# An output projection cut into Strassen units for all four blocks, with a shorter feature map and numerators divided on GpSimd

## The chip, the cores and the metric

The kernel runs on one core of a Trainium2 chip. The metric is device time in microseconds (us) of one execution, lower is better. The engines are called PE (TensorE, the matmuls), PEld (its weight loads), DVE (VectorE), ACT (ScalarE), POOL (GpSimd) and SP (SyncE, which here issues most DMAs).

## The reference

Two functions share one normalised input of 2048 tokens by 1024 features:

```python
def reference(A_x, A_wqkv, A_wo, B_x, B_w_gate, B_w_up, B_w_down):
    def _A_ref(x, wqkv, wo):                      # linear attention, H = 32 heads of Dh = 32
        qkv = ...(x @ wqkv)
        phi = lambda t: jnp.where(t > 0, t + 1, jnp.exp(t)) + 1e-6
        pq, pk = phi(q), phi(k)
        kv = jnp.einsum("bhsd,bhse->bhde", pk, v)
        z = jnp.einsum("bhsd->bhd", pk)
        num = jnp.einsum("bhqd,bhde->bhqe", pq, kv)
        den = jnp.einsum("bhqd,bhd->bhq", pq, z)[..., None] + 1e-6
        return (num / den) @ wo                   # heads put side by side again
    def _B_ref(x, w_gate, w_up, w_down):
        g = _silu(x @ w_gate)
        u = x @ w_up
        return (g * u) @ w_down
    x = A_x
    xn = _layernorm(x, axis=-1)
    s = _A_ref(xn, A_wqkv, A_wo)
    g = _silu(_B_ref(xn, B_w_gate, B_w_up, B_w_down))   # F = 3584
    return x + s * g
```

## The kernel before

The 2048 tokens are 16 tiles of 128, or 4 blocks `b` of 512 (four tiles `t` each). The order of instructions on PE, DVE, ACT and POOL, and later on SP, is the order in which the Python code emits them (`manual_schedule`); nothing is reordered. An engine that waits therefore holds up everything emitted behind it.

**Stage 1 (0 to about 128 us).** Per tile, layer norm, a transpose to `xnT`, four products of 8 matmuls each into `kv_ps` (L528; two chunks of keys, two of values), the feature map of the keys (`emit_phi`, L145), and the sums `kvz` over tokens.

**Stage 2 (128 to 244 us).** For each block, eight query products `q_ps` (`emit_Q`, L178, 8 matmuls each), whose feature map goes to `pqT`. When a block's `pqT` is whole, its four tiles get `nd` (`emit_ND`, L707): 8 short matmuls for numerators and denominators. DVE adds the epsilon and inverts the denominators (`rden`), multiplies the numerators by them out of PSUM into a tile `o_blk` (L729), and SP transposes `o_blk` into `oT` by DMA (`emit_OT`, L735). From `oT` the output projection `s` is made: for blocks 0 and 1 directly (`emit_S`, 8 matmuls for each half of the columns, so 16 per tile), for blocks 2 and 3 in Strassen-Winograd units (`s_unit`, L767). A unit takes two tiles and makes seven products (x, w, y, x2, z, z2, w2) of 4 matmuls each, 28 instead of 32. It needs four sums of `oT` (`sums`, on DVE), four sums of the weight (`To`, 16 POOL operations at L762, emitted ahead of block 1's queries), and copies between PSUM banks by ACT.

**What sets the order in stage 2.** The queries of block b+1 are emitted while block b's tiles are finished: `run(body, at, b)` emits the items of `body` and puts one `nd` after each item whose index is in `at`. In blocks 2 and 3 the query items are mixed with direct projections. Query and projection products share five PSUM banks (tag "B2"); `nd` has a single buffer (tag "A"), so one `nd` waits until the one before it has been read. `o_blk` has four buffers, so tile t of block 1 waits for the transpose of tile t of block 0. `oT` has two.

**Weight preparation.** In stages 1 and 2 a pipeline (`prep_step`, L324) also prepares weights of the second function: load, an ACT square for a scale, a DVE scaling in place (L283, 128x2048 bf16) and four POOL sums (`emit_T`, L295 to L298), then a store. One step is taken at fixed places of stage 1, two in block 0's queries, and one with each `nd` of blocks 1 and 2.

**Stage 3 (244 us to the end).** Two passes of gate and up products (L939) and down products (L1124), all in the same seven-product form. Weights that were not prepared earlier go through the same square, scaling and sums during the first pass.

Of the kernel before, what the change touches and what calls it, by code (L numbers as in the profile page):

```python
# [21 lines left out]
def kernel(  # L22
# [39 lines left out]
    NPREP = 13  # L62
# [82 lines left out]
    def emit_phi(work, t_ps, dst, W, in_place=False, act=False):  # L145
        e_t = work.tile([P, W], FP32, name="e_t", tag="e_t")
        if act:
            nc.scalar.activation(out=e_t[:], in_=t_ps, func=ACT.Relu, scale=-1.0)
            nc.scalar.activation(out=e_t[:], in_=e_t[:], func=ACT.Exp, scale=-1.0)
            nc.scalar.activation(out=t_ps, in_=t_ps, func=ACT.Relu)  # L150
            phi_late.append(lambda: nc.vector.scalar_tensor_tensor(out=dst, in0=e_t[:], scalar=EPS, in1=t_ps,
                                                                   op0=ALU.add, op1=ALU.add))
            return
        nc.scalar.activation(out=e_t[:], in_=t_ps, func=ACT.Exp)
        if in_place:
            r = t_ps
            nc.vector.tensor_scalar(out=r, in0=t_ps, scalar1=0.0, scalar2=EPS, op0=ALU.max, op1=ALU.add)
        else:
            r_t = work.tile([P, W], FP32, name="r_t", tag="r_t")
            r = r_t[:]  # L160
            nc.scalar.activation(out=r, in_=t_ps, func=ACT.Relu)
            nc.vector.tensor_scalar(out=r, in0=r, scalar1=EPS, scalar2=None, op0=ALU.add)
        nc.vector.scalar_tensor_tensor(out=dst, in0=e_t[:], scalar=1.0, in1=r,
                                       op0=ALU.min, op1=ALU.add)

# [12 lines left out]
    def emit_Q(b, g, act=None):  # L178
        pqT = pqT_of(b)
        btok = slice(b * TB, (b + 1) * TB)  # L180
        q_ps = ps2.tile([P, TB], FP32, name="q_ps", tag="B2")
        for dc in range(DC):
            nc.tensor.matmul(q_ps[:], lhsT=wq_sb[:, dc, g * P:(g + 1) * P], rhs=xn_ap(dc, btok),  # L183
                             start=(dc == 0), stop=(dc == DC - 1))
        emit_phi(phiw, q_ps[:], pqT[:, g, :], TB, in_place=True, act=b > 0 if act is None else act)
# [132 lines left out]
    prep_q = deque(gkeys[2:2 + 2 * NPREP:2] + wkeys[0:NWE - 2] + gkeys[0:2] + wkeys[NWE - 2:NWE])  # L318
# [44 lines left out]
    with ExitStack() as p1:  # L363
# [169 lines left out]
        def emit_Bev(i, c):  # L533
# [5 lines left out]
            if c < NCC:  # L539
                emit_phi(phiw, kv_ps[:], pk_sb[:, c * CW:(c + 1) * CW], CW, in_place=i >= 9)  # L540
# [126 lines left out]
        for g in range(1, G):  # L667
            emit_Q(0, g, act=g in (3,5,7))
            if g in (2, 5):
                prep(1)  # L670
            phi_flush()
# [4 lines left out]
    s_sums = {}  # L676

# [18 lines left out]
    with ExitStack() as p2:  # L696
# [10 lines left out]
        def emit_ND(b, t, nd):  # L707
# [18 lines left out]
            for j in range(NJ):  # L726
                g0 = j * GPT
                ng = min(GPT, G - g0)
                nc.vector.tensor_tensor(  # L729
                    out=o_sb[:, g0 * P:(g0 + ng) * P].rearrange("p (g h e) -> p g h e", g=ng, h=HPG),  # L730
                    in0=nd[:, j, 0:ng, 0:P].rearrange("p g (h e) -> p g h e", h=HPG),
                    in1=rden[:, g0:g0 + ng, :, None].to_broadcast([P, ng, HPG, DH]),
                    op=ALU.mult)
# [6 lines left out]
        def emit_S(b, t, cc, bank=None):  # L740
            oT = oT_tiles[b]
            ttok = slice(t * P, (t + 1) * P)
            if (b, t) not in s_tiles:
                s_tiles[(b, t)] = work.tile([P, D], BF16, name="s_sb", tag="s_sb")
            s_sb = s_tiles[(b, t)]
            s_ps = bank or ps2.tile([P, CW], FP32, name="s_ps", tag="B2")
            for c in range(G):
                mm = nc.tensor.matmul(s_ps[:], lhsT=oT[:, c, ttok], rhs=wo_sb[:, c, cc * CW:(cc + 1) * CW],  # L748
                                      start=(c == 0), stop=(c == G - 1))
                marks.setdefault(("S", b, t), mm)  # L750
            nc.scalar.activation(out=s_sb[:, cc * CW:(cc + 1) * CW], in_=s_ps[:], func=ACT.Copy, scale=s_sc[:])
            if cc == NCC - 1:
                r0 = b * TB + t * P
                nc.scalar.dma_start(out=s_dram[r0:r0 + P, :], in_=s_tiles.pop((b, t))[:])

        To_sb = tp.tile([P, 4, HG, CW], F16, name="To_sb")
        To = [To_sb[:, k] for k in range(4)]
# [9 lines left out]
        def s_unit(b, u):  # L767
# [8 lines left out]
            X, Y, Z, W = fx[n % 2], fx[1 - n % 2], fx[2], fx[3 + n % 2]  # L776
            so = wq_sb[:, TPB:DC, :].rearrange("p a b -> p (a b)")[:, (n % 2) * 2048:(n % 2) * 2048 + 3 * HG * P]
            so = so.bitcast(F16).rearrange("p (q k t) -> p q k t", q=3, k=HG)
# [60 lines left out]
        def s_item(b, t, cc):  # L839
            return lambda: emit_S(b, t, cc)  # L840

        def nd_item(b, t):
            def f():
                raw, nd = psa_tile("nd")

                def nd_ot():
                    emit_ND(b, t, nd)
                    emit_OT(b, t)
# [6 lines left out]

        def mix(a, b_):
            r = []
            for k in range(max(len(a), len(b_))):
                r += a[k:k + 1] + b_[k:k + 1]
            return r  # L860

        def sh(b, hf):
            return [s_item(b, t, cc) for t in (2 * hf, 2 * hf + 1) for cc in range(NCC)]
# [11 lines left out]
        run(qs(1), (1, 3, 5, 7), 0)  # L875
        q = qs(2)
        run(q[:2] + mix(q[2:], sh(0, 0) + sh(0, 1)), (1, 4, 7, 10), 1)
        q = qs(3)
        run(q[:2] + mix(q[2:], sh(1, 0)), (1, 4, 7, 10), 2, (0, 2, 1, 3))
        nds = [nd_item(3, t) for t in (0, 2, 1, 3)]  # L880
        emit_S(1, 2, 0)
        emit_S(1, 2, 1)
        fx.extend([ps2.tile([P, CW], FP32, name="fx%d" % k, tag="B2") for k in range(5)])
        units = [s_unit(2, 0), s_unit(2, 1)]
        u = units[0]
        nds[0]()
        u["x"]()
        u["sums"]()
        emit_S(1, 3, 0, fx[4])
        nds[1]()  # L890
        emit_S(1, 3, 1, fx[2])
        u["w"]()
        units[1]["sums"]()
        u["y"]()
        u["x2"]()
        nds[2]()
        u["z"]()
        parts = []
        for n in range(1, 4):
            u, v = units[n - 1], units[n]  # L900
            for st in ('x w nd new -z2 sums y -w2 x2 z', 'x w new Ssum -z2 sums p y -w2 x2 z p', 'x w -z2 y p -w2 z x2 p z2 silu w2')[n - 1].split():
                if st == "nd":
                    nds[3]()
                elif st == "new":
                    units.append(s_unit(3, n - 1))
                elif st == "sums":
                    units[n + 1]["sums"]()
# [4 lines left out]
                elif st == "Ssum":  # L912
                    blk_es.close()
                    blk12_es.close()
                    sp = ctx.enter_context(tc.tile_pool(name="p3S", bufs=1, side="right", reuse_waits="tile"))
                    emit_Ssum(passes[0], parts)
                    stat_ps[0] = lambda: psa_tile("st_ps3")[0][:, 0, 511:512]
                    prep_flush()
                elif st[0] == "-":
                    u[st[1:]]()  # L920
                else:
                    v[st]()
# [3 lines left out]
    with ExitStack() as p3:  # L926
# [358 lines left out]
        for pi, p in enumerate(passes):  # L1285
# [20 lines left out]
            def pipe2(j):  # L1306
                if raw(j):
                    t = w_tiles[keys[j]]
                    emit_st2(keys[j], t, later=j == n - 1)
                    emit_lk(keys[j][2])  # L1310
# [124 lines left out]
```

## Time and profile before

| | |
|---|---|
| time, median of 3 runs | 758.13 us (757.99 to 758.14) |
| span of the profiled execution | 756.7 us |
| median less span | 1.4 us |
| PE busy in the span | 746.6 us (99%) |
| DVE, ACT, POOL busy | 558.5, 376.3, 278.4 us |
| mean granted TensorE clock | 0.999 |

The answers list no time for the profiled execution beside its span; 1.4 us is what the median of the timed runs has above it. The span runs from the first to the last instruction. A busy PE is a PE with a matmul in its pipeline, and is not by that at its peak rate.

### The profile page before, as it was taken

What the parts mean: (1) busy time and instruction counts of PE and PEld (TensorE: products, weight loads), DVE (VectorE), ACT (ScalarE), POOL (GpSimd) and SP (SyncE); (2) the same over time, 40 slices, a digit from 0 to 9 for tenths busy, and PEclk for the clock granted to TensorE, in tenths of its full rate; (3) what the DMA queues carried; (4) which work ended last, traced back from release to release, by engine and by line L of the source; (5) the groups of instructions that cost most, each with busy time, mean ns of one, the idle gap of its engine ahead of it and who ended that gap; (6) DMA issues with size and microseconds to landing.
All of it is one profiled execution on the core that took longest, in us unless ns stands there. A gap on an engine that the chain in (4) does not pass through costs nothing.

```text
span 756.7 us, 10426 instructions
## 1 busy us (share of the span) xinstructions
PE 746.6 (99%) x3662; PEld 349.0 (46%) x3731; DVE 558.5 (74%) x1031; ACT 376.3 (50%) x526; POOL 278.4 (37%) x352
## 2 busy tenths in 40 slices
PE   8999999999999999999999999999999999999997
PEld 4544544454454444444444444444444444444443
DVE  6687787896697788888889775368676777787335
ACT  5677776889956565666659311132322223211122
POOL 2444799998540276868585000100000000200000
PEclk9999999999999999999999999999999999999999
DMA  9968799879679668878799236398644445530824
GB/s 316 295 149 146 223 334 300 302 137 307 201 180 298 229 217 292 309 268 312 278 329 408 86 121 239 124 377 321 229 174 167 167 168 173 180 133 15 283 83 135
DMA packets 105845, 170.30 MB, mean 225 GB/s; under 512 B 34816, under 2 KB 82176, under 8 KB 95168
## 3 DMA queue, kind: packets, MB, share of 16 engines
q1 hardware_dynamic: 100144, 144.99, 59.3%
q0 software_dynamic: 4208, 22.15, 7.5%
q10 hardware_dynamic: 1440, 2.49, 0.9%
q8 instruction: 29, 0.48, 0.3%
q14 instruction: 24, 0.20, 0.1%
HBM read 111.67 MB, written 50.59 MB: 214 GB/s over the span
## 4 chain that ended last, share of the span: by engine, by line
PE 97%; DVE 1%; ACT 1%; issue 1%; ACTq 0%; DVEq 0%
PE zw L939 26%; PE kv_ps L528 15%; PE xb L939 13%; PE dzw L1124 12%; PE yb L939 6%; PE q_ps L183 6%; PE dx L1124 6%; PE dy L1124 3%; PE fx L790 3%; PE s_ps L748 2%; PE kvz L550 1%; PE nd L717 1%; PE df L1124 1%; PE warm_ps L564 1%; DVE w_sb L283 0%
## 5 line engine op out<-in xcount | busy, mean ns | idle before, releaser
L939 PEld LDWEIGHTS <-w_sb 128*128 128x128 f16 (+1 forms) x1568 | 152.1, 98 | 182.7
L939 PE MATMUL xb<-xnT,w_sb 128*128 128x512 bf16 x420 | 113.3, 379 | 1.5
L528 PE MATMUL kv_ps<-wkv_sb,xnT 128*128 128x512 bf16 x499 | 112.9, 379 | 1.1 <-DVE xnT L515 0.3
L939 PE MATMUL zw<-xnT,w_sb 128*128 128x512 bf16 x448 | 105.8, 379 | 0.0
L939 PE MATMUL zw<-S,w_sb 128*128 128x512 f16 x448 | 105.8, 379 | 0.0
L295 POOL TENSOR_TENSOR w_sb<-w_sb 128x512 f16<-128x512 bf16 x42 | 50.2, 1195 | 95.7 <-DVE w_sb L283 51.3
L260 ACT ACTIVATE w_sb<-w_sb 128x2048 bf16<-128x2048 bf16 x42 | 79.9, 1902 | 4.4 <-DMA w_sb<-in_B_w_up_dram 4.4
L1124 PE MATMUL dx<-w_sb,hT 128*128 128x512 bf16 x202 | 76.6, 379 | 0.3
L528 PEld LDWEIGHTS <-xnT 128*128 128x128 bf16 x512 | 48.4, 98 | 55.9 <-ACT xnT L517 0.8
L1124 PEld LDWEIGHTS <-hT 128*128 128x128 bf16 (+1 forms) x462 | 44.7, 98 | 52.4
L183 PE MATMUL q_ps<-xnT,wq_sb 128*128 128x512 bf16 x249 | 58.0, 379 | 0.4
L1015 ACT ACTIVATE sg<-cg 128x1024 bf16<-128x1024 f32 x28 | 29.6, 1057 | 57.4 <-DVE cg L1008 57.4
L939 PE MATMUL yb<-S,w_sb 128*128 128x512 f16 x224 | 57.4, 378 | 0.1
L1124 PE MATMUL dzw<-w_sb,hT 128*128 128x512 f16 (+1 forms) x190 | 57.0, 379 | 0.0
L1008 DVE SCALAR_TENSOR_TENSOR cg<-zw,rc_all,s 128x1024 f32<-128x1024 f32 x28 | 35.9, 1284 | 25.5 <-PE zw L939 13.8
L967 DVE SCALAR_TENSOR_TENSOR s<-yb,rc_all,s 128x512 f32<-128x512 f32 x42 | 31.5, 749 | 28.1 <-ACT s L966 28.1
L296 POOL TENSOR_TENSOR w_sb<-w_sb 128x512 f16<-128x512 bf16 x42 | 50.5, 1201 | 3.3
L1064 POOL TENSOR_TENSOR hs<-hT 128x512 f16<-128x512 bf16 x2 | 2.5, 1250 | 132.6 <-ACT sg L1015 132.6
L298 POOL TENSOR_TENSOR w_sb<-w_sb 128x512 f16<-128x512 bf16 x42 | 50.2, 1196 | 0.0
L297 POOL TENSOR_TENSOR w_sb<-w_sb 128x512 f16<-128x512 bf16 x42 | 50.2, 1195 | 0.0
L1098 POOL DMA_DIRECT2D out_dram<-io x16 | 8.7, 542 | 101.9 <-DVE io L1097 101.6
L966 ACT ACTIVATE s<-xb,rcl 128x512 f32<-128x512 f32 x14 | 9.6, 687 | 65.3 <-PE xb L939 65.3
(179 smaller groups left out, 1187.4 us busy)
## 6 DMA issues: line engine op xcount, KB each, us to landing
w_sb<-pk_g SPq DMA_DIRECT2D x27, 1024.0 KB, 6.3
pk_g<-w_sb SPq DMA_DIRECT2D x14, 1024.0 KB, 5.0
w_sb<-wd SPq DMA_DIRECT2D x14, 1024.0 KB, 6.0
w_sb<-pk_u SPq DMA_DIRECT2D x14, 1024.0 KB, 5.0
pk_u<-w_sb POOLq DMA_DIRECT2D x13, 1024.0 KB, 5.3
w_sb<-wd SPq DMA_DIRECT2D x14, 768.0 KB, 4.8
w_sb<-in_B_w_gate_dram SPq DMA_DIRECT2D x14, 512.0 KB, 6.7
w_sb<-in_B_w_down_dram SPq DMA_DIRECT2D x28, 256.0 KB, 4.9
```

The source lines that it names most:

```text
L183: nc.tensor.matmul(q_ps[:], lhsT=wq_sb[:, dc, g * P:(g + 1) * P], rhs=xn_ap(dc, btok), start=(dc == 0), stop=(dc == DC - 1))
L260: nc.scalar.activation(out=junk, in_=raw_view(key, t), func=ACT.Square, accum_out=asum[:])
L295: nc.gpsimd.tensor_tensor(out=T1, in0=b12, in1=b11, op=ALU.subtract)
L296: nc.gpsimd.tensor_tensor(out=T2, in0=b22, in1=T1, op=ALU.subtract)
L297: nc.gpsimd.tensor_tensor(out=T3, in0=b22, in1=b12, op=ALU.subtract)
L298: nc.gpsimd.tensor_tensor(out=T4, in0=b21, in1=T2, op=ALU.subtract)
L528: mm = nc.tensor.matmul(kv_ps[:], lhsT=xn_ap(dc, tok), rhs=wkv_sb[:, dc, c * CW:(c + 1) * CW], start=(dc == 0), stop=(dc == DC - 1))
L939: mm = nc.tensor.matmul(out, lhsT=lhs(k), rhs=rhs(k), start=(first and k == 0), stop=(k == HK - 1), skip_group_check=True)
L967: nc.vector.scalar_tensor_tensor(out=s2[:], in0=y_[:], scalar=rc, in1=s1[:], op0=ALU.mult, op1=ALU.add)
L1008: nc.vector.scalar_tensor_tensor(out=d12, in0=zw[:], scalar=rc, in1=s2[:, None, :].to_broadcast([P, 2, TB]), op0=ALU.mult, op1=ALU.add)
L1015: nc.scalar.activation(out=sg[:, 1:3, :], in_=cf[:], func=ACT.Silu)
L1124: nc.tensor.matmul(out, lhsT=lhs, rhs=rhs, start=first, stop=lastk, skip_group_check=True)
```

## The change

Four things are changed.

- The feature map has one form for queries and keys: ACT takes the exponential into a bf16 tile, DVE caps it and adds epsilon there (SBUF to SBUF, bf16), and DVE takes the larger of it and `t + 1 + EPS` (one operand in PSUM). Before, there were three forms. In stage 1's tiles below 9, ACT also took a Relu into SBUF, and DVE had one operation on it and one to combine. From tile 9 on, and for five query products of block 0, DVE had two operations, both on PSUM. For the other 27 query products ACT had three operations and DVE one.
- All four blocks are projected by units. Block 0's two units follow block 2's queries without anything between them; the six others follow block 3's queries.
- For the odd tiles of blocks 0 to 2 and all tiles of block 3, ACT copies the numerators out of PSUM into `o_blk`, and one POOL operation (128x1024) multiplies them by `rden` in place.
- Gate weights 11 and 12 are no longer prepared in stages 1 and 2, but in stage 3's first pass. Two buffers move: `so_sb` gets its own place, and `To[2]` is written over a part of the weight.

On the engines, as built: PE loses 16 matmuls of 128x512 (128 direct ones go, 112 in units come). ACT loses 27 times two operations of the query map and 18 Relus. DVE gets a second operation in 27 query maps and 16 more unit sums, and loses 30 numerator products. POOL gets ten products of 128x1024; they stand behind the 16 operations of the weight sums and between the `emit_T` groups.

```diff
-    NPREP = 13
+    LATE_G = (11, 12)
...
-    def emit_phi(work, t_ps, dst, W, in_place=False, act=False):
-        e_t = work.tile([P, W], FP32, name="e_t", tag="e_t")
+    def emit_phi(work, t_ps, dst, W, act=False):
+        e_t = work.tile([P, W], FP32 if act else BF16, name="e_t", tag="e_t")
...
         nc.scalar.activation(out=e_t[:], in_=t_ps, func=ACT.Exp)
-        if in_place:
-            r = t_ps
-            nc.vector.tensor_scalar(out=r, in0=t_ps, scalar1=0.0, scalar2=EPS, op0=ALU.max, op1=ALU.add)
-        else:
-            r_t = work.tile([P, W], FP32, name="r_t", tag="r_t")
-            r = r_t[:]
-            nc.scalar.activation(out=r, in_=t_ps, func=ACT.Relu)
-            nc.vector.tensor_scalar(out=r, in0=r, scalar1=EPS, scalar2=None, op0=ALU.add)
-        nc.vector.scalar_tensor_tensor(out=dst, in0=e_t[:], scalar=1.0, in1=r,
-                                       op0=ALU.min, op1=ALU.add)
+        nc.vector.tensor_scalar(out=e_t[:], in0=e_t[:], scalar1=1.0, scalar2=EPS, op0=ALU.min, op1=ALU.add)
+        nc.vector.scalar_tensor_tensor(out=dst, in0=t_ps, scalar=1.0 + EPS, in1=e_t[:], op0=ALU.add, op1=ALU.max)
...
-    prep_q = deque(gkeys[2:2 + 2 * NPREP:2] + wkeys[0:NWE - 2] + gkeys[0:2] + wkeys[NWE - 2:NWE])
+    prep_q = deque([k for k in gkeys[2::2] if k[2] not in LATE_G] + wkeys[0:NWE - 2] + gkeys[0:2] + wkeys[NWE - 2:NWE])
...
             for j in range(NJ):
                 g0 = j * GPT
                 ng = min(GPT, G - g0)
+                if split:
+                    nc.scalar.copy(out=o_sb[:, g0 * P:(g0 + ng) * P].rearrange("p (g c) -> p g c", g=ng),
+                                   in_=nd[:, j, 0:ng, 0:P])
+                    continue
                 nc.vector.tensor_tensor(
...
+            if split:
+                ov = o_sb.rearrange("p (h e) -> p h e", e=DH)
+                nc.gpsimd.tensor_tensor(
+                    out=ov, in0=ov,
+                    in1=rden[:, 0:G, :].rearrange("p g h -> p (g h)")[:, :, None].to_broadcast([P, G * HPG, DH]),
+                    op=ALU.mult)
...
-        To_sb = tp.tile([P, 4, HG, CW], F16, name="To_sb")
-        To = [To_sb[:, k] for k in range(4)]
+        To_sb = tp.tile([P, 3, HG, CW], F16, name="To_sb")
+        To = [To_sb[:, 0], To_sb[:, 1], wo_sb[:, 0:HG, CW:D].bitcast(F16), To_sb[:, 2]]
+        so_sb = tp.tile([P, 2, 3, HG, P], F16, name="so_sb")
...
-                    emit_ND(b, t, nd)
+                    emit_ND(b, t, nd, split=b == NB - 1 or t % 2 == 1)
...
-        run(qs(1), (1, 3, 5, 7), 0)
-        q = qs(2)
-        run(q[:2] + mix(q[2:], sh(0, 0) + sh(0, 1)), (1, 4, 7, 10), 1)
-        q = qs(3)
-        run(q[:2] + mix(q[2:], sh(1, 0)), (1, 4, 7, 10), 2, (0, 2, 1, 3))
...
+        run(qs(1), (1, 3, 5, 7), 0)
+        run(qs(2), (1, 3, 5, 7), 1)
+        fx_new()
+        q = qs(3)
+        unit(0, 0)["sums"]()
+        steps(None, (0, 0), (0, 1), 'x w sums y x2 z')
+        steps((0, 0), (0, 1), None, 'x w -z2 y -w2 x2 z')
+        steps((0, 1), None, None, 'q -z2 -w2')
+        run(q, (1, 3, 5, 6), 2, (0, 2, 1, 3))
+        fx_new()
+        unit_n[0] = 0
+        order_u = [(1, 0), (1, 1), (2, 0), (2, 1), (3, 0), (3, 1)]
+        unit(1, 0)["sums"]()
+        for n, text in enumerate(('x w sums y x2 z', 'x w -z2 sums y -w2 x2 z', 'x w nd -z2 sums y nd -w2 x2 z',
+                                  'x w nd -z2 y nd -w2 x2 sums z', 'x w Ssum -z2 sums p y -w2 x2 z p',
+                                  'x w -z2 y p -w2 z x2 p z2 silu w2')):
+            steps(order_u[n - 1] if n else None, order_u[n], order_u[n + 1] if n < 5 else None, text)
...
-                    emit_lk(keys[j][2])
+                    if keys[j][1] == "u":
+                        emit_lk(keys[j][2])
```

In `steps`, a bare name is a step of the unit in hand, a name with "-" one of the unit before it, "sums" those of the unit after it, "nd" the next tile of block 3, and "q" one query product.

## The prediction

> **What bounds the kernel now.** I read the page's busy line and chain first, then PE's waits, then stage 2 engine by engine.
>
> ```profile
> PE 746.6 (99%) x3662; PEld 349.0 (46%) x3731; DVE 558.5 (74%) x1031; ACT 376.3 (50%) x526; POOL 278.4 (37%) x352
> ...
> PE 97%; DVE 1%; ACT 1%; issue 1%; ACTq 0%; DVEq 0%
> ...
> PE warm_ps L564 <- DVE warm L561: 1.5, 1, 1.5
> PE nd L264 <- ACT w_sb L260: 0.3, 1, 0.3
> PE kv_ps L528 <- DVE xnT L515: 0.3, 1, 0.3
> PE kv_ps L528 <- ACT xnT L517: 0.3, 1, 0.3
> ```
>
> PE carries 97% of the chain, and its waits add up to 2.4 us, 0.3 of them in stage 2 (the last numbers are us in total, times, longest). So a matmul that goes is worth its full time, and there is next to no wait to win back: every new wait of PE is a loss. The averages of the others hide stage 2:
>
> ```profile
> 140.00:160.00 20.00, 19.85 (x114) 9.91 (x115) 16.92 (x40) 18.68 (x33) 19.84 (x18) 1.00 0.74 198
> 160.00:180.00 20.00, 19.62 (x118) 9.91 (x118) 17.45 (x38) 17.46 (x27) 17.32 (x16) 1.00 0.90 230
> 180.00:200.00 20.00, 19.89 (x106) 9.59 (x106) 12.30 (x34) 18.22 (x30) 13.44 (x12) 1.00 0.76 237
> ```
>
> The windows' columns are length, then PE, PEld, DVE, ACT, POOL, clock, DMA. POOL, at 37% overall, is full from 140 to 160. Its timeline and two of DVE's:
>
> ```profile
> 149.29 1.16 POOL L298 TENSOR_TENSOR w_sb<-w_sb 128x512 f16<-128x512 bf16 x1
> 150.41 4.50 POOL L762 TENSOR_TENSOR To_sb<-wo_sb 128x512 f16<-128x512 bf16 x4
> 154.85 4.51 POOL L762 TENSOR_TENSOR To_sb<-wo_sb,To_sb 128x512 f16<-128x512 bf16 x4
> 159.30 4.51 POOL L762 TENSOR_TENSOR To_sb<-wo_sb 128x512 f16<-128x512 bf16 x4
> 163.76 4.50 POOL L762 TENSOR_TENSOR To_sb<-wo_sb,To_sb 128x512 f16<-128x512 bf16 x4
> ...
> 163.25 1.35 DVE L729 TENSOR_TENSOR o_blk<-nd,rden 128x384 bf16<-128x384 f32 x3
> ...
> 165.13 3.67 DVE L283 TENSOR_SCALAR w_sb<-w_sb,cs_all 128x2048 bf16<-128x2048 bf16 x1
> ...
> 179.26 0.75 DVE L283 TENSOR_SCALAR w_sb<-w_sb,cs_all 128x2048 bf16<-128x2048 bf16 x1
> ...
> 161.62 0.63 PE L717 MATMUL nd<-KVZ,pqT 128*128 128x132 bf16 x8
> ...
> oT<-o_blk SPq DMA_TRANSPOSE x12, 4.2
> ```
>
> POOL works without a pause from 84.55 (first weight sum) to 168.26 (last `To`). Nobody waits for that, because the next user of `To` is a unit at 219. The same DVE scaling took 0.75 us with POOL idle and 3.67 while POOL ran `To`. PE's row at 161.62 is block 1's first `nd`. The last row (from the DMA answer) gives 4.2 us from issue to landing of a transpose.
>
> **The change part by part.**
>
> *PE.* Eight matmuls take 1.73 us in the chain, 0.216 each. 16 go: -3.5 us. If all else kept up: 758.1 - 3.5 = 754.6, or 754.3 with stage 2's wait of 0.3.
>
> *Feature map.* Clean DVE cost per product, start to start: an SBUF operation of 512 (0.43 for the fp32 one, 0.41 for a norm of 512; 0.37 taken for bf16) plus the combine, 0.61: 0.98. Before, 27 query products cost DVE 0.61 and ACT 1.73 (three operations), the others DVE 1.34. In stage 1, DVE's new pair stands beside 7.4 us of PE per tile, and before, the form with its bank freed by DVE already ran there without a PE wait: nothing, 0 to 1 if a bank is late.
>
> *The new SBUF operation meets POOL.* The scaling's 16 runs beside POOL that I measured from 84 to 212 lasted mostly 0.9 to 1.7 us against 0.75, each ending about 0.5 us after a POOL operation. So an operation of this kind waits for the running POOL operation to end, 0 to 1.15, and I take 0.4. POOL then lost 0.33 to 0.45 itself; the new operation has a quarter of the elements, so I take 0.05 (0 to 0.45). The Trainium skill, SBUF — State Buffer, Who interferes with whom, says that VectorE in a two-port mode and GpSimd exclude each other for a whole instruction, which speaks against putting bf16 work on DVE beside POOL. By that rule no wait outlasts one POOL operation, 1.15 here. The 3.67 row differs: it sat through the ends at 166.0 and 167.1 and finished 0.55 after the last `To`; the row stands, and it is a rival below.
>
> *Numerators.* As built, the first POOL product (block 0, tile 1) stands behind all 16 `To` operations. SP's transpose of that tile waits for it. Tile 1 of block 1 needs the same `o_blk` buffer, so its ACT copies wait for the transpose, and behind these copies ACT holds the exponentials of the next queries. Call C the time at which the copies may start:
> - end of `To`: 168.3 before. About 30 new SBUF operations fall in 84 to 170 (14 keys, 16 queries), 30 x 0.05 = 1.5: 169.8 (168.3 to 181.8).
> - POOL product of 1024: twice the 1.15 of 512, 2.3 (1.15 to two slow ones of 1.6, 3.2): 172.1.
> - transpose 4.2 (its rows: 3.1 to 6.9): C = 176.3 (172.6 to 191.9).
>
> PE would be at that tile at 161.62 + 0.47 (the `nd`) + 2 x 1.73 = 165.6, so the copies are 10 us late. This is the step that decides.
>
> *From C to the first unit.* Nothing is queued between block 2's queries and unit (0,0) now, and its product w needs a sum that DVE does last. After C, in order: three copies 1.3 (two of 512 took 1.27), exponential 0.6, two feature maps 1.96, `nd` (1,2) on DVE 2.06 (0.37+0.35+1.35, overlapped), preparation step 1.28 (0.61 + 0.67 pitch), two feature maps 1.96, denominators of (1,3) 0.79, step 1.28, sum 0.42: 11.65. Waits for POOL add 4 x 0.4 + 2 x 0.5 + 0.4 = 3.0. So w starts at 176.3 + 14.6 = 190.9 (184.2 clean and with the low C; 206.5 with the high one). PE without waits: 161.62 + 0.47 + 6 x 1.73 + 3 x 0.49 + 0.87 = 174.8. Loss 16.1 (9.4 to 31.7). Even with C at once, DVE alone is late: block 2's queries put 8 x 0.98 + 2 x 2.06 + 2 x 0.79 + 4 x 1.28 = 18.7 us clean on DVE, against 8 x 1.73 + 4 x 0.49 = 15.8 on PE. From block 1's last map (159.4) that reaches w at about 180.6, a loss of 5.8. Before, 16 direct products (27.6 us for the two blocks' 128 matmuls) stood between them and let DVE catch up.
>
> *Block 0's units.* DVE does all eight sums ahead of z's read; 0 clean, 2 with waits: 0.5.
>
> *Block 3's queries to unit (1,0).* DVE 7.84 + 5.7 + 2 x 1.28 = 16.1 clean, 19 with waits, against PE's 15.8, then a sum of 0.42: loss 0.6 to 3.7, taken 2.
>
> *Block 3's tiles.* Copies 1.3, POOL 2.3, transpose 4.2 for each tile, while PE has 6 us per unit; the last pair's sums come due 9.6 us after its `nd`, and those 7.8 us queue behind another tile's: 0 to 2.5, taken 0.5.
>
> *Weights 11 and 12 in stage 3.* Two more POOL groups of 4.7, two squares (2.1) and two scalings (0.75 to 1.5) over four slots of 6.05 us, in windows with POOL at 12 to 17 and DVE at 16 to 17.5 of 20: the cover is the lead of two slots; 0, up to 1.5 if it is used up. POOL loses as much in stage 2.
>
> Sum: -3.5 - 0.3 + 16.1 + 0.5 + 2 + 0.5 = +15.3, on the span 756.7 + 15.3 = 772.0; the median stands 1.4 above the span: **773.4**.
>
> **The rivals.**
>
> 1. *PE's cut is paid in full* (the other side). It needs w(0,0) within 3.8 us of 174.8, so C at or before 178.6 - 11.65 = 167.0. For it: PE never waits now, and ACT loses 1.2 us in each of 27 maps. Against it: the `To` chain alone ends at 168.3, and DVE's 18.7 exceeds 15.8. It gives 754.3 to 757: 5%.
> 2. *POOL's products come early, DVE alone is late.* If C does not bind, the loss is 5.8 + 0.6, less 3.8: 760.7. For it: the sum above; against it: the order on POOL as built. 5%.
> 3. *DVE is shut out for the whole `To` run*, as in the 3.67 row. Block 1's maps then start at 168.3: + 13.5 (8 x 0.98 + 5.7) + 18.7 + 4 of waits and sum: w at 204.5, loss 29.7, + 2 - 3.8: 786. For it: two ends of POOL operations were passed over; against it: beside the weight sums DVE got in at the next end. 10%.
> 4. The main course: 80%.
>
> **How the numbers follow.** The likeliest is the main course, 773.4. Its own bounds go with C: low 758.1 - 3.8 + 9.4 + 0.6 = 764.3; high, with C at 186 (ten of the 13.5 us of POOL delays) about 784. The range 764 to 786 holds it and rival 3, and leaves out rivals 1 and 2 and the worst sum. About 0.2% (1.5 us) is what a measurement of this kernel can tell from no change. Faster: rival 1's lower end, 0.04. Same: its rest, 0.02. Slower: all else, 0.94.
>
> **What would show it.** Right: ACT idle ahead of the copies of `nd` into `o_blk`, put down to a DMA of `oT`, at 165 to 177; PE idle ahead of an `nd` for ACT, and ahead of the unit's second product for a DVE sum, together above 10 us; stage 3 starting near 256 instead of 244.4; POOL's product of 1024 at about 2.3 us. Wrong: PE's waits in stage 2 below 5 us; the `To` run over before 165; or DVE, not ACT's copies, behind the idle time from 165 to 177, which is rival 3. A loss after 260 would mean that weights 11 and 12 are not covered.

## The result: 5.5% slower, and 26.5 us more than predicted

The changed kernel takes 799.94 us (median of 4 runs, 798.38 to 800.99) against 758.13 us: a ratio of 1.0548, 95% interval 1.0533 to 1.0563. The direction is the predicted one, the size is not: 41.8 us lost instead of 15.3, and the range ended at 786.

The profiled execution has a span of 796.6 us, 39.9 more than before. Two marks on PE split it. The first gate product of stage 3 starts at 269.18 instead of 244.43 (+24.75). The first down product starts at 454.26 instead of 414.15 (+40.11). The rest runs as before. So stage 2 loses 24.75 us, the first gate and up pass 15.4, and the second loss is one that the prediction had put at 0.

**The profile after.** The busy line and the chain from the page:

```profile
PE 752.8 (95%) x3646; PEld 348.8 (44%) x3715; DVE 580.6 (73%) x1052; ACT 353.7 (44%) x492; POOL 295.9 (37%) x364
...
PE 80%; POOL 8%; DVE 5%; issue 4%; DMA 1%; ACT 1%; SPq 0%; POOLq 0%; ACTq 0%; DVEq 0%
```

The averages of the other engines do not betray the loss: DVE is at 73% as against 74%, POOL at 37% in both. It is in the chain, where PE falls from 97% to 80%, and in PE's waits (us in total, times, longest):

```profile
PE yb L923 <- POOL w_sb L287: 10.0, 2, 5.1
PE fx L776 <- DVE so_sb L769: 9.7, 3, 6.9
PE nd L255 <- DVE tot L260: 6.1, 3, 3.1
```

The first line is stage 3: a gate or up product waits for a weight sum on POOL. The second is a unit's product that waits for DVE's sum, the third a tile's `nd` behind DVE. The windows (columns as before) show where:

```profile
160.00:180.00 20.00, 14.78 (x87) 7.54 (x89) 17.01 (x36) 11.55 (x19) 19.92 (x16) 0.92 0.38 96
180.00:200.00 20.00, 11.17 (x48) 4.63 (x48) 18.41 (x34) 7.53 (x13) 16.87 (x14) 0.82 0.81 238
...
220.00:240.00 20.00, 14.56 (x76) 6.88 (x79) 15.62 (x34) 10.12 (x20) 9.78 (x8) 1.00 0.57 159
...
400.00:420.00 20.00, 14.74 (x64) 6.37 (x64) 13.85 (x26) 8.20 (x10) 16.20 (x17) 0.91 0.76 247
420.00:440.00 20.00, 14.97 (x58) 6.27 (x58) 11.44 (x25) 7.31 (x8) 13.20 (x14) 0.83 0.95 366
```

Every other window after 20 us and before the end has PE at 17.9 or more. The clock, 1.00 throughout these stages before, is at 0.82 to 0.92 in four of the five. The step that the prediction hung on is there too, in ACT's, POOL's and DVE's timelines:

```profile
175.98 1.14 ACT L722 CAST o_blk<-nd 128x384 bf16<-128x384 f32 x3 [4.42 <-POOL w_sb L287]
...
169.27 4.22 POOL L732 TENSOR_TENSOR o_blk<-o_blk,rden 128x1024 bf16<-128x1024 bf16 x2
...
175.45 0.37 DVE L713 TENSOR_SCALAR rden<-nd,rc_all 128x24 f32<-128x24 f32 x2
```

POOL's first division starts at 169.27 behind the weight sums (169.8 predicted), and the copies of block 1's tile 1 at 175.98 after 4.42 us of idle time (C was put at 176.3). Whether the transpose is what held them is another matter: DVE's row ends just before the copies start. The trace and the runs answer it below.

### The profile page after: what moved, and what is told of

The parts are those of the page before. It is cut to its first block, busy times and chain, and to the rows that moved or that the text cites. A ratio compares the mean times of both kernels' runs of the same rounds, so it can differ in the third digit from the quotient of the medians.

```text
span 796.6 us, 10431 instructions
## 1 busy us (share of the span) xinstructions
PE 752.8 (95%) x3646; PEld 348.8 (44%) x3715; DVE 580.6 (73%) x1052; ACT 353.7 (44%) x492; POOL 295.9 (37%) x364
## 4 chain that ended last, share of the span: by engine, by line
PE 80%; POOL 8%; DVE 5%; issue 4%; DMA 1%; ACT 1%; SPq 0%; POOLq 0%; ACTq 0%; DVEq 0%
PE zw L923 22%; PE kv_ps L519 13%; PE dzw L1108 11%; PE xb L923 11%; PE yb L923 6%; PE dx L1108 6%; PE fx L776 5%; PE dy L1108 3%; POOL To_sb L749 2%; POOL w_sb L287 2%; POOL w_sb L286 1%; POOL w_sb L289 1%; PE kvz L541 1%; DVE w_sb L274 1%; DMA w_sb<-in_B_w_gate_dram 1%
## 5 line engine op out<-in xcount | busy, mean ns | idle before, releaser
L923 PE MATMUL xb<-xnT,w_sb 128*128 128x512 bf16 x421 | 114.9, 383 | 1.9 <-ACT sg L998 0.5
L923 PE MATMUL zw<-xnT,w_sb 128*128 128x512 bf16 (+1 forms) x447 | 105.8, 379 | 0.1
L286 POOL TENSOR_TENSOR w_sb<-w_sb 128x512 f16<-128x512 bf16 x42 | 50.9, 1211 | 97.1 <-DVE w_sb L274 61.0
L923 PE MATMUL yb<-S,w_sb 128*128 128x512 f16 x224 | 59.2, 387 | 10.2 <-POOL w_sb L287 10.0
L155 DVE TENSOR_SCALAR e_t<-e_t 128x512 bf16<-128x512 bf16 x64 | 36.9, 577 | 25.2 <-ACT e_t L154 25.2
L287 POOL TENSOR_TENSOR w_sb<-w_sb 128x512 f16<-128x512 bf16 x42 | 51.4, 1225 | 3.3
L288 POOL TENSOR_TENSOR w_sb<-w_sb 128x512 f16<-128x512 bf16 x42 | 51.2, 1220 | 0.0
L289 POOL TENSOR_TENSOR w_sb<-w_sb 128x512 f16<-128x512 bf16 x42 | 50.3, 1197 | 0.0
```

The costliest lines, as they stand in the source:

```text
L155: nc.vector.tensor_scalar(out=e_t[:], in0=e_t[:], scalar1=1.0, scalar2=EPS, op0=ALU.min, op1=ALU.add)
L286: nc.gpsimd.tensor_tensor(out=T1, in0=b12, in1=b11, op=ALU.subtract)
L287: nc.gpsimd.tensor_tensor(out=T2, in0=b22, in1=T1, op=ALU.subtract)
L288: nc.gpsimd.tensor_tensor(out=T3, in0=b22, in1=b12, op=ALU.subtract)
L289: nc.gpsimd.tensor_tensor(out=T4, in0=b21, in1=T2, op=ALU.subtract)
L923: mm = nc.tensor.matmul(out, lhsT=lhs(k), rhs=rhs(k), start=(first and k == 0), stop=(k == HK - 1), skip_group_check=True)
```

## The experiments

Below, "second product" is the start of the first unit's second product on PE, the one that waits for DVE's sum: 174.8 with no wait, 190.9 predicted, 193.1 measured in the changed kernel. "Pass" is the time from the first gate product to the first down product: 169.7 us before, 185.1 in the changed kernel. Each mark comes from one profiled execution. In the changed kernel the second product is steady: e2 and e5, whose edits bear mostly on what comes later, have it at 193.4 and 193.2.

| run | median us | ratio, 95% interval | second product | stage 3 starts | pass |
|---|---|---|---|---|---|
| changed kernel | 799.9 | 1.053 to 1.056 | 193.1 | 269.2 | 185.1 |
| e1, before with late weights | 773.1 | 1.018 to 1.021 | | 243.7 | 185.5 |
| e2, late weights 7 and 10 | 794.6 | 1.047 to 1.050 | 193.4 | 270.0 | 180.6 |
| e5, no late weight | 793.3 | 1.045 to 1.048 | 193.2 | 279.0 | 170.7 |
| e3, block 0 on DVE | 797.6 | 1.050 to 1.054 | 191.3 | 267.5 | 185.6 |
| e4, map in fp32 | 806.1 | 1.061 to 1.065 | 198.1 | 276.4 | 185.9 |
| e8, no weight sums | 795.8 | 1.048 to 1.051 | 189.1 | 265.6 | 186.2 |
| e10, old query map | 802.2 | 1.056 to 1.059 | 195.6 | 271.8 | 185.1 |
| e11, preparation moved | 799.3 | 1.053 to 1.056 | 184.5 | 270.2 | 185.4 |
| e16, no preparation | 788.7 | 1.039 to 1.043 | 187.1 | 260.7 | 186.7 |
| e13, extra matmuls | 800.7 | 1.053 to 1.057 | 194.0 | 270.1 | 186.1 |
| e6, relieved queries | 773.6 | 1.018 to 1.022 | 176.3 | 258.9 | 170.9 |
| e7, GpSimd clear of the units | 782.1 | 1.030 to 1.033 | 186.0 | 267.1 | 170.1 |
| e14, e6 without sums | 767.9 | 1.011 to 1.014 | 176.4 | 253.1 | 169.9 |
| e15, e6 without preparation | 764.7 | 1.007 to 1.011 | 176.4 | 248.9 | 171.1 |
| e12, half of the cut | 768.9 | 1.013 to 1.016 | | 252.6 | 169.9 |

**Stage 3: the late weights (e1, e2, e5).**

```diff
e1, in the kernel before:
-    NPREP = 13
+    LATE_G = (11, 12)
...
+                    if keys[j][1] == "u":
                         emit_lk(keys[j][2])
e2, in the changed kernel:  LATE_G = (7, 10)
e5, in the changed kernel:  LATE_G = ()
```

> The kernel before with only one part of the change: gate weights 11 and 12 left to stage 3. Theory: in stage 3 the sums of a weight stand on POOL only one slot of 6.06 us ahead of their first product, and the change makes five keys in a row (up 10, gate 11, up 11, gate 12, up 12) need them, with two down-weight groups between: seven POOL groups of about 5.7 us in about four slots. So the whole loss of stage 3 seen in the changed kernel (15.4 us) returns here: about 773 us (771 to 775), with PE waiting for a POOL sum twice. Rival, the view of the prediction: the lead covers it, 758 to 760. Second rival: the loss comes only because the changed kernel reaches stage 3 with its weight loads late: then also 758 to 760 here.

Measured: 773.08 us, the theory's number. PE's waits hold the changed kernel's line once more, on a kernel whose stage 2 is untouched:

```profile
PE yb L939 <- POOL w_sb L296: 10.2, 3, 5.1
```

POOL's timeline of the changed kernel shows why; the rows are the stores with which each group of four sums ends:

```profile
395.75 0.57 POOL L304 DMA_DIRECT2D pk_u<-w_sb  x1 [0.30 <-POOL w_sb L289]
...
401.96 0.57 POOL L300 DMA_DIRECT2D wd<-w_sb  x1
...
408.34 0.55 POOL L304 DMA_DIRECT2D pk_g<-w_sb  x1 [0.30 <-POOL w_sb L289]
...
413.84 0.57 POOL L304 DMA_DIRECT2D pk_u<-w_sb  x1 [0.30 <-POOL w_sb L289]
...
422.24 0.57 POOL L304 DMA_DIRECT2D pk_g<-w_sb  x1 [0.30 <-DMA io<-in_A_x_dram]
...
427.40 0.57 POOL L300 DMA_DIRECT2D wd<-w_sb  x1
...
433.44 0.55 POOL L304 DMA_DIRECT2D pk_u<-w_sb  x1 [0.30 <-POOL w_sb L289]
```

That is up 10, a down weight, gate 11, up 11, gate 12, a down weight, up 12: seven groups of 5.5 to 6.7 us between 390.8 and 434, with 2.9 us of idle time ahead of gate 12. PE wants a key every 6.06 us. A slot i of the pass ends with the group for key i + 3, and the first products of that key (`emit_a`) open slot i + 2: one slot lies between, not two, and nothing is left over when two groups fall into one slot.

> The changed kernel with gate weights 7 and 10 left to stage 3 in place of 11 and 12. The work is the same; a down-weight group follows every third key, and around gates 7 and 10 none falls between the three neighbouring keys. Theory (demand of POOL in a row of slots decides): three groups, 13.4 us until the needed sum, against two slots and some slack, 13.5: nearly no loss, 784 to 787 us. Rival (each gate weight left late costs 7 us of POOL wherever it stands): 799 to 801, no change.

Measured: 794.61 us; 4.5 us of the pass come back instead of 13 to 16. No product waits for a POOL sum any more, so that part of the theory held. In its place PE waits 6.2 us behind ACT:

```profile
PE xb L923 <- ACT sg L998: 6.2, 2, 3.3
...
339.39 1.91 ACT L251 ACTIVATE w_sb<-w_sb 128x2048 bf16<-128x2048 bf16 x1 [2.67 <-DMA w_sb<-in_B_w_gate_dram]
```

The raw gate weight is loaded into a weight buffer that a down weight's store (5.5 us) still held; SP issues the load at 335.12, it lands 4.2 us later, and ACT's square, first in its queue, holds the SiLU behind it that PE needs. A late gate weight costs 5 to 8 us either way.

> The changed kernel with no gate weight left late (11 and 12 are prepared in stages 1 and 2 again; the preparation has enough steps for it, one store falls to the flush at the end of stage 2). Theory: both things that cost time in stage 3 (the POOL sums that come due too close, and the raw gate load that waits for a weight slot) go, and stage 3 takes as long as before: 799.9 - 15.4 = 784.6 us (784 to 786). Rival: two more weights in stage 2 cost there what they save later, as POOL and DVE are full there: 788 to 800.

Measured: 793.29 us. The pass is back at 170.7, so the late weights are the whole of stage 3's loss. But stage 3 starts 9.8 us later: the two weights now fall into block 3's queries, and the wait for the sums ahead of unit (1,0) grows from 2.0 to 7.2 us. The rival was right on the total.

**Stage 2: one part at a time (e3, e4, e8, e10, e11, e16, e13).**

```diff
e3:
-                    emit_ND(b, t, nd, split=b == NB - 1 or t % 2 == 1)
+                    emit_ND(b, t, nd, split=b == NB - 1 or (t % 2 == 1 and b > 0))
e4:
-        e_t = work.tile([P, W], FP32 if act else BF16, name="e_t", tag="e_t")
+        e_t = work.tile([P, W], FP32, name="e_t", tag="e_t")
```

> The changed kernel with block 0's tiles 1 and 3 divided on VectorE as before, so that no transpose of block 0 waits for GpSimd behind the weight sums of the projection. Theory (that wait, through the four o_blk buffers, holds ScalarE's copies of tile 1 of block 1, and the first unit): the first unit's second product starts near 185 instead of 193, with 2.5 us more on VectorE in block 1's queries: 790 to 794 us. Rival (VectorE beside a full GpSimd is the bound in any case, the wait only one of several that end together): 797 to 802.

Measured: 797.55 us. The transpose that tile 1 of block 1 needs is long done, its copies start at 174.04, right behind DVE's denominators (173.60, 0.37 us), and the second product moves by 1.9 us only. The rival held: DVE is late by nearly as much for its own reasons. (The 1.9 us are a net figure, as e3 also gives DVE more work in block 1's queries.)

> The changed kernel with the exponential's tile in fp32 in place of bf16, nothing else. Theory (the map's new operation is held up by GpSimd only because its bf16 form cannot run beside a GpSimd operation): its time is 0.43 us everywhere, with none of 2.00, and 3 to 6 us of the loss between 145 and 193 go: 794 to 797 us. Rival (fp32 from SBUF to SBUF is held up in the same way, or the wait is not of this kind): 799 to 802, and durations from 0.5 to 2 us stay.

Measured: 806.13 us; slower, and against the theory. The map's SBUF operation between 84 and 200, by form, in the changed kernel and in e4:

```profile
L155 DVE TENSOR_SCALAR e_t<-e_t 128x512 bf16<-128x512 bf16 x36 | 26.9, 747 | 7.5 <-ACT e_t L154 7.5
...
L155 DVE TENSOR_SCALAR e_t<-e_t 128x512 f32<-128x512 f32 x36 | 31.7, 881 | 7.4 <-ACT e_t L154 7.4
```

747 ns beside POOL is the 0.37 + 0.4 of the prediction. The waiting is not one of bf16: fp32 waits as long and works longer.

```diff
e8, in prep_step:
-            emit_T(*k3, later=True)
+            pass
e10:
-            return lambda: emit_Q(b, g)
+            return lambda: emit_Q(b, g, act=True)
...
-            emit_Q(0, g)
+            emit_Q(0, g, act=g in (3, 5, 7))
e11:
-                if 0 < b < NB - 1:
+                if (b, t) == (2, 0):
...
-        steps(None, (0, 0), (0, 1), 'x w sums y x2 z')
-        steps((0, 0), (0, 1), None, 'x w -z2 y -w2 x2 z')
+        steps(None, (0, 0), (0, 1), 'x w P sums y x2 z')
+        steps((0, 0), (0, 1), None, 'x w P -z2 y -w2 x2 P z')
...
(P is one preparation step; three more stand in units (1,0), (1,1), one in (2,0))
e16: squares, scalings and sums are skipped for SKIP = set(list(prep_q)[-5:])
```

> The changed kernel without the four GpSimd sums of each weight that is prepared in stages 1 and 2 (they are left out; the projection's own sums, the divisions and stage 3's sums stay). Theory (VectorE's operations from SBUF to SBUF, and the divisions, wait for these GpSimd operations): VectorE in block 2's queries falls to its clean 18.7 us, and of the 25 us lost in stage 2 only 5 to 9 stay; stage 3's 15 us stay: 779 to 785 us. Rival (VectorE's own work is the bound whatever GpSimd does): 793 us or more.

Measured: 795.81 us, the second product at 189.1. POOL is idle for 6 to 9 us ahead of each of its divisions there, and 21 of 25 us stay. The theory fell: leaving these sums out brings back 4 us of the loss. What holds the rest this run does not show; the projection's own sums and the divisions still stand on POOL in it.

> The changed kernel with the query map of before (three ScalarE operations and one on VectorE for blocks 1 to 3 and three products of block 0), nothing else undone. Theory (a query block without direct products has no room on either engine): VectorE falls to 15.7 us in block 2's queries, but ScalarE rises to 13.8 + 2.3 for copies + 8.4 for squares = 24.5 against 15.8 of the matmul engine, so block 1's queries come on time and block 2's do not: 787 to 794 us. Rival (the short map is the main cause in stage 2): 778 to 784.

Measured: 802.19 us, above both. Block 1's queries come on time, as expected. Then a single DVE scaling takes 7.05 us (DVE's and POOL's rows):

```profile
165.95 7.05 DVE L274 TENSOR_SCALAR w_sb<-w_sb,cs_all 128x2048 bf16<-128x2048 bf16 x1
...
164.22 4.50 POOL L749 TENSOR_TENSOR To_sb<-wo_sb,To_sb 128x512 f16<-128x512 bf16 x4
168.66 3.80 POOL L732 TENSOR_TENSOR o_blk<-o_blk,rden 128x1024 bf16<-128x1024 bf16 x2
```

It starts inside the `To` run and ends 0.5 us after the two divisions: it got in at none of the ends between. At the end of the chain behind it, tile (1,1)'s copies start at 177.26 and PE waits 8.3 us for the next `nd`. (Block 0's transpose for that buffer, issued at 170.6 behind POOL's division, landed at 173.8 and would have held those copies to about then in any case.) Later in the block ACT is late, with squares and copies.

> The changed kernel with seven of the eight preparation steps of blocks 1 and 2 moved into the units, nothing else. Theory (work only changes its place: the queries of block 2 are relieved of 5.1 us on VectorE, the units get VectorE sums of 1.3 us beside GpSimd in place of 0.42): the first unit's second product starts near 186 instead of 193, and the units give it back: 794 to 804 us. Rival (the preparation steps in the queries are the main cause, and the units have room): 784 to 790.

Measured: 799.25 us. The second product comes at 184.5, 8.6 us earlier, and stage 3 starts 1.0 us later than in the changed kernel: the units gave it all back, as the theory said.

> The changed kernel with the last five weights of the preparation only loaded and stored (five squares, scalings and groups of sums fewer in blocks 1 to 3's queries). Theory (short map, numerators and preparation together overfill the queries; no one of them alone): 3.4 us less on VectorE and ScalarE per step, but the wait of block 1's copies for block 0's transposes and the map stay: 786 to 793 us. Rival (the preparation alone is what overfills them): 774 to 781, that is the 15 us of stage 3 and no more.

Measured: 788.68 us, within the theory's range: the preparation in the queries is 8.5 of stage 2's 24.75 us, not the whole. (The marks are those of a run of 791.45 us, 2.8 above the median.)

```diff
e13:
+        def dummy():
+            d_ps = ps2.tile([P, TB], FP32, name="d_ps", tag="B2")
+            for dc in range(DC):
+                nc.tensor.matmul(d_ps[:], lhsT=wq_sb[:, dc, 0:P], rhs=xn_ap(dc, slice(0, TB)), ...)
...
-        run(qs(2), (1, 3, 5, 7), 1)
+        run(qd(2), (1, 5, 9, 13), 1)      # qd: a dummy ahead of each query product but the first two
```

> The changed kernel with six extra products of 8 matmuls between block 2's queries whose results nobody reads: 6 x 1.73 = 10.4 us more for the matmul engine, nothing for the others. Theory (the matmul engine is not the bound there; VectorE, ScalarE and GpSimd are): next to nothing is added, 797 to 802 us, perhaps less than the changed kernel because the granted clock does not fall. Rival (the matmul engine's time still counts): 808 to 811.

Measured: 800.69 us: 0.75 us for 10.4 us of matmuls, less than the runs of either kernel differ among themselves. The same window in the changed kernel and in e13:

```profile
165.00:185.00 20.00, 13.78 (x80) 6.81 (x81) 17.82 (x38) 12.46 (x18) 19.84 (x15) 0.91 0.65 177
...
165.00:185.00 20.00, 19.89 (x113) 9.79 (x113) 17.68 (x37) 10.79 (x17) 19.84 (x15) 1.00 0.66 151
```

PE goes from 13.78 to 19.89 of 20 us, DVE and POOL do the same work in the same time. In block 2's queries the matmuls that the change removed were worth nothing.

**Several parts together (e6, e7, e14, e15, e12).**

```diff
e6, against the changed kernel: LATE_G = (); query map as in e10; preparation as in e11; and
-                    emit_ND(b, t, nd, split=b == NB - 1 or t % 2 == 1)
+                    emit_ND(b, t, nd, split=False)
...
-        run(qs(2), (1, 3, 5, 7), 1)
+        b2 = qs(2)
+        b2.insert(7, lambda: u_sums(0, 0))
+        run(b2, (1, 3, 5, 6), 1)
...
+        q.insert(6, lambda: u_sums(1, 0))
-        run(q, (1, 3, 5, 6), 2, (0, 2, 1, 3))
+        run(q, (0, 2, 4, 5), 2, (0, 2, 1, 3))
```

> All four blocks by units as in the changed kernel, but with what stood beside the query products taken off: the queries of blocks 1 to 3 and three of block 0 with the map of before (three ScalarE operations, one on VectorE), all numerators on VectorE, no late gate weight, seven of the eight preparation steps of blocks 1 and 2 moved into the units, and the first unit's sums of blocks 0 and 1 emitted ahead of the last query. VectorE then has 8 x 0.61 + 4 x 2.06 = 13.1 us in a block's queries and ScalarE 13.8, against 15.8 of the matmuls. Theory (the changed kernel loses because a query block without direct products has more work on VectorE and GpSimd than on the matmul engine): the cut of 16 matmuls is paid nearly in full, 754 to 757 us, below the kernel before. Rival (the units themselves cannot follow the queries without an idle time, whatever stands beside them): 760 to 768.

Measured: 773.62 us, above both ranges. The second product comes at 176.3, 1.5 us after the ideal, so the first handover is repaired. The units are not: stage 3 starts at 258.9. DVE's and POOL's rows in the first unit:

```profile
176.27 0.42 DVE L764 TENSOR_TENSOR so_sb<-so_sb,oT 128x512 f16<-128x512 f16 x1
...
179.75 1.26 DVE L764 TENSOR_TENSOR so_sb<-so_sb,oT 128x512 f16<-128x512 f16 x1
...
180.80 1.22 POOL L287 TENSOR_TENSOR w_sb<-w_sb 128x512 f16<-128x512 bf16 x1
```

The same sum takes 0.42 us with POOL idle and 1.26 beside it: the engines take turns, one operation each.

```diff
e7, against e6:
-    PREP_AT = ((4, 1), (5, 1), (6, 1), (7, 1))
+    PREP_AT = ((4, 1), (4, 3), (5, 1), (5, 3), (6, 1), (6, 3), (7, 1), (7, 3))
...
+        PREP_ND = ((0, 1), (1, 1), (2, 0), (2, 1))     # and no P in the units
...
+        b2.insert(6, lambda: u_sums(0, 0))
+        run(b2, (0, 2, 4, 7), 1)
e14: emit_T is left out for the steps after block 2's queries
e15: squares, scalings and sums are skipped for SKIP = set(list(prep_q)[-7:])
```

> As e6_covered, but no weight preparation stands in the units, so that GpSimd is idle there: four preparation steps move to tiles 4 to 7 of stage 1, one to block 1's queries, one to block 2's, two to block 3's; one query in eight takes the short map; the sums of the first unit stand one query earlier, and the tiles of a block keep two queries between them. Theory (in e6_covered VectorE's sums took 1.26 to 1.39 us beside GpSimd in place of 0.42, which made the units the bound): the sums take 0.42 again, PE's idle time in the units is under 4 us, 754.5 to 758 us. Rival (the units are late for another reason, their copies or their single banks): 760 to 768.

> A second look at e7_pool_clear for the steadiness of its stages: the same as e7_pool_clear by either theory, within 1 us.

Measured: 782.14 us, and 782.02 when it was run again. Against both views: stage 1 has no room for four more steps either (block 0's queries start at 135.1 instead of 127.9), POOL carries its backlog to 190, and the early sums, now in block 2's queries, take 1.14 to 1.37 us there. The marks are less steady here: the second product is at 186.0 in the one profile and at 189.6 in the other, block 0's queries start at 135.1 and 136.7.

> As e6_covered (773.6 us), but the GpSimd sums of the weights prepared after block 2's queries are left out, so that GpSimd has no work in the units; ScalarE's squares and VectorE's scalings stay. Theory (the 15 us that e6_covered still loses come from VectorE's sums beside GpSimd, 1.3 us in place of 0.42): 757 to 763 us. Rival (the preparation's own VectorE and ScalarE work or the units' handovers): 767 to 773.

Measured: 767.92 us, at the lower edge of the rival's range. The sums take 0.42 us, and 5.7 us come back; ACT's squares of 2.1 us among the units' copies stay.

> As e6_covered (773.6 us), but the last seven weights of the preparation are only loaded (whole) and stored: their squares, scalings and sums are left out, so that neither block 2's or 3's queries nor the units hold any of that work. Theory (the 16 direct products that went were the room for the preparation, and the units have none): with the room no longer asked for, only the short idle times at the tiles' denominators stay, about 5 us: 757 to 762 us. Rival (the units lose by their own handovers): 765 to 768, as with the sums alone left out (767.9).

Measured: 764.72 us, between the two ranges, just below the rival's. What is missing to a cut paid in full (754.3) goes from 13.6 to 10.4 us. Of these, 2.8 lie at one unit that waits for transposes behind a weight's store on SP, and 4.6 are six waits of 0.7 to 0.9 us from start to start, four at `nd`s that follow each other too closely and two at a unit's second product. The rest was not taken further.

```diff
e12, against e6: block 0 projected by emit_S as before, between block 2's queries; units for blocks 1 to 3
+        sh = [(lambda t=t, cc=cc: emit_S(0, t, cc)) for t in range(4) for cc in range(NCC)]
+        body = q[:2]
+        for k in range(8):
+            body += q[2 + k:3 + k] + sh[k:k + 1]
...
+        body.append(prep_item)
+        run(body, (1, 4, 7, 10), 1)
...
+        PREP_ND = ((0, 1), (1, 0), (1, 1), (1, 2), (1, 3), (2, 0))
```

> Half of the cut, with cover: block 0 is projected directly, its eight products between block 2's queries as before; blocks 1 to 3 by units, so 8 matmuls go instead of 16. Map of before but for two products, numerators on VectorE, no late gate weight, preparation in the queries of blocks 1 and 2, the third weight sum on GpSimd after block 0's products, the sums of unit (1,0) ahead of the last query. Theory (units cost nothing where the queries before them have cover or are relieved): 758.3 - 1.7 = 756.6 plus up to 2 for the one uncovered handover: 756.5 to 758.8. Rival (each uncovered handover costs 5 or more): 762 to 766.

Measured: 768.94 us, against the theory. Block 2's queries, with cover, lose nothing between 165 and 189; the idle time is around block 1's (two waits, 1.5 us) and in block 3's queries (two, 2.3), which have none, and in the units (six, 5.6). Its stages in the table are those of a run of 766.97 us. No version that was run beats the kernel before.

## Why the prediction was right in direction and wrong in size

| step of the sum | predicted | measured |
|---|---|---|
| 16 matmuls and 0.3 us of waits go | -3.8 | nothing against it, taken as -3.8 |
| copies of tile (1,1) may start (C) | 176.3 | the transpose landed at 174.42, the copies started at 175.98 |
| second product of the first unit | 190.9, loss 16.1 | 193.1, loss 18.3 |
| from there to unit (1,0)'s second product | 0.5 + 2 | 229.2 - 193.1 = 36.1 against 27.9 of products: 8.2 |
| from there to stage 3 | 0.5 | 269.2 - 229.2 = 40.0 against 37.4: 2.6 |
| weights 11 and 12 | 0, up to 1.5 | 15.4 |

(27.9 is 14 unit products of 0.865, 8 query products of 1.73 and four tiles of 0.49; 37.4 is 41 unit products and four tiles.) The last column adds up to 40.7, within 1 us of the span's 39.9.

**The failed step is "Weights 11 and 12 in stage 3".** Its cover, "the lead of two slots", is one slot in the code's order, and it was weighed against averages over 20 us. The rows of the kernel before spoke against it. From 366.09 to 395.71 POOL makes the sums of five weights (up 10, a down weight, up 11, a down weight, up 12), and two pauses of 0.9 us are nearly all that is left between them:

```profile
378.20 1.15 POOL L295 TENSOR_TENSOR w_sb<-w_sb 128x512 f16<-128x512 bf16 x1 [0.93 <-ACT sg L1015]
...
390.25 1.15 POOL L295 TENSOR_TENSOR w_sb<-w_sb 128x512 f16<-128x512 bf16 x1 [0.89 <-issue]
```

Two more groups of 4.7 us do not fit there; the long pauses of the same windows, 6.8 and 6.1 us, lie ahead of 366.09 and behind 395.71. The demand had to be counted key by key. e1 shows 14.8 us for this part alone, where the sum had 0; e5 shows that without it the pass takes 170.7. This is the loss after 260 that the prediction named as a sign against the cover.

**The second miss is the size of "Block 3's queries to unit (1,0)" and what follows it.** Two reasons are shown. DVE's 16.1 us were counted as if nothing else stood in the chain; in the trace the last queries' exponentials stand on ACT behind copies that wait for DVE's denominators, and each side waits for the other:

```profile
224.72 1.14 ACT L722 CAST o_blk<-nd 128x384 bf16<-128x384 f32 x3 [4.25 <-DVE rden L713]
...
226.39 0.69 DVE L155 TENSOR_SCALAR e_t<-e_t 128x512 bf16<-128x512 bf16 x1 [1.36 <-ACT e_t L154]
```

PE waits 1.3, 2.5 and 1.8 us there. And PE's clock was in no term: after 7 us without a matmul, 193 to 205 us ran at a granted clock of 0.82, which is about 2 us of the 8.2. In e1, where PE waits 10.7 us in the pass, the pass is 15.8 longer; most of what exceeds the waits, 4.5 us, is slower matmuls right behind the two long ones.

**C was right as a time and wrong as the cause; that the time fits is luck.** Tile (0,1)'s transpose, issued at 171.21, landed at 174.42, and the copies did not start then. They started at 175.98, when DVE had written the denominators of tile (1,1) (175.45 to 175.82). Tile (1,3) shows the same order with a buffer that had been free for 11 us; there the profile's chain itself goes from DVE's denominators to the copies:

```profile
187.82 0.38 DVE rden L713 x2
...
188.35 1.15 ACT o_blk L722 x3
```

In e3, with no transpose to wait for, they again follow the denominators. (The label of the row at 175.98, a weight sum on POOL, names what ended last nearby; the copies use nothing of it.) The two paths ended 1.4 us apart, so taking the transpose away could not gain much.

So rival 2, "DVE alone is late", is the course that was taken, and its 760.7 was far too low. It let DVE start at 159.4, called the end of block 1's last map, and reach the second product at about 180.6 (its own terms, 159.4 + 18.7 + 0.42, make 178.5). In the traces that map ends at 161.27 before and at 163.37 in the changed kernel; blocks 0 and 1's own queries had been charged with nothing. From 163.37 DVE takes 29.7 us to the end of the sum at 193.07. At the prediction's clean prices 19.9 of these are work (18.7, one more pair of denominators, 0.79, and the sum). Three waits for ACT are 3.3. The 6.5 left over, a difference and not a measured wait, are operations that took longer than the prediction's clean time: two of the map's SBUF operations took 2.00 us beside POOL, the sum 2.13 instead of 0.42; the main course had allowed 3.0 for this from C on. That no part alone carries the loss is what e3, e8, e10, e11 and e16 show: taking one away brings the second product forward by 1.9 to 8.6 us, or, with the old map (e10), puts it back by 2.5, and the total changes by between +2.3 and -11.3 us.

**Rival 3, DVE shut out for the whole `To` run,** did not happen in the changed kernel, where the map's SBUF operations beside the `To` run took 0.52 to 0.68 us. In e10 one scaling took 7.05 us. Why that one was passed over and the others were not is not shown.

**Where the expected gain went:** the 16 direct products had been the time in which DVE, ACT and POOL finished the maps, the numerators and the preparation. e13 shows that PE's time there is free. With map and numerators as before, no late weight and the preparation moved (e6), then without its sums (e14), then without all of it (e15), the loss against before shrinks to 15.4, 9.4 and 6.6 us. That is the part of it which is shown; why the rest stays, 10 us of a cut paid in full, is open beyond the waits named at e15.

## What to carry to other kernels

Before work is taken from the engine that sets the time, look at what the others do beside it: count their work over the stretch that becomes shorter, in program order, and ask which of them is next. A pipeline that prepares operands is judged by its busiest row of slots and by the place of each step in the queue, not by its share of a window; a step with a lead of one slot has no room for a second group. And where an engine's wait is taken as the cause because its time fits, take it away once: here the fitting wait was worth 2 of 25 us.

## What the runs showed of the hardware

**A DVE operation can be shut out by a row of POOL operations.** 0.75 us became 7.05 in e10 and the wait passed over several ends of POOL operations; for short operations beside weight sums the two engines alternate (0.42 to 1.26 us in e6). The Trainium skill, SBUF — State Buffer, Who interferes with whom, says that both an operation of VectorE with two SBUF inputs and a single-input one in a two-port mode share a port pair with GpSimd, and that the one that comes second is blocked for the other's whole instruction. The sums agree with it, and e4 agrees that fp32 is no way out (0.88 us on average as against 0.75 in bf16). The 7.05 us of e10 are longer than any one POOL operation beside it (1.15 and 1.9 us); there the measurement decides: this operation was not let in after one of them.

**Idle time on PE is paid more than once.** In the changed kernel's second long wait in stage 3, PE is idle for most of the first row; in the second it is busy all the time, at little more than half speed:

```profile
425.00:431.00 6.00, 1.02 (x7) 0.39 (x6) 4.28 (x13) 0.00 (x0) 5.91 (x8) 0.86 0.98 393
431.00:437.00 6.00, 6.00 (x16) 2.22 (x17) 0.75 (x1) 2.34 (x2) 2.69 (x3) 0.57 0.86 348
```

The Trainium skill, TensorE: Matmul & The Clock Gate, Part 1, has the clock halved after an idle window of about 3.4 us, for about as long; an estimate from that is 1.7 us for each wait above this length. In e1 the four products behind each long wait, 3.46 us at full speed, took 5.15 us after the first (5.06 us of idle time) and 6.24 us after the second (4.97): 1.7 and 2.8 us on top. The first agrees with the estimate, the second is above it.
